# First expert's share added in mid-pass, decodes kept off one change of pass, one sum kept in PSUM, and an earlier load of the tail's tokens

## The chip, the cores and the metric

The kernel runs on one core of one Trainium2 chip. The metric is the device time of one execution in microseconds (us). The kernel before took 1981.72 us, the median of three runs (1981.59 to 1982.14).

## The reference

Three layers follow each other. Block-causal attention over 4 batches of 8 heads, 576 positions and width 64 gives 2304 tokens of width 512. A mixture of 8 experts follows: a gate matrix P comes from eight rounds of row and column normalising, and each expert adds its weighted output:

```python
for e in range(E):
    h = np.maximum(x @ w1[e], 0.0)
    ye = h @ w2[e]
    out += P[:, e:e + 1] * ye
```

A last layer computes `h = x @ w_in`, a softmax of h times h, a normalisation scaled by `g_ln`, and a product with `w_out`. The inputs `w_in`, `w_out` and `g_ln` belong to this last layer.

## The kernel before

All products are made from two parts of each number, a rounded high part and the rest, so that one product takes three matmuls. Expert 0 is computed beside the attention. Its result y, not yet weighted, is held in DRAM (`ydram`) for the last 1536 tokens.

Experts 1 to 7 are split in halves, the units u = 2 to 15, and the tokens are worked in three **passes** of 768 tokens, p = 0, 1 and 2. In every unit the first layer is a fast 2x2 product scheme: seven half-size products instead of eight, named "1" to "7" (`first_layer`, L712). Their sums are formed by VectorE in banks a, b and c of PSUM, for two column groups g. Here `plus` (L717) adds a PSUM bank and a saved tile, and writes to a new SBUF tile or to a given place. For product "5" it writes a tile `vu3` in SBUF, and `hidden` (L759, in pass 0 L748) reads that tile.

In passes 1 and 2 the second layer uses seven products as well. `weighted_hidden` (L755) multiplies by the gate weights `Pb`, forms seven operand tiles R with differences on GpSimd and VectorE (L773) and splits them in two parts (ScalarE L769, GpSimd L770). `second_products` (L804) then makes the seven products of the unit before, and VectorE adds each into a running sum, `summed(f)` (L816; the first unit copies on ScalarE, L814). All of these sums stay in SBUF for a whole pass. TensorE has six PSUM banks of the pool `l1p` for the banks a, b and c and for three of four second-layer outputs (`yps`), and two banks of `mm`.

At the end of a pass `finish_pass` (L827) combines the seven sums by seven adds (L831, four on VectorE and three on GpSimd). It then loads the four blocks of y from `ydram` (L846), weights them on GpSimd (L848), adds them on VectorE (L850) and stores the result to `rdram` (L851). It runs once pass 1 is complete, when unit 2 of pass 2 is already under way, and once at the end of pass 2. The new pass cannot overwrite a sum before that sum has been combined and stored.

The weights of the last layer arrive as 64-bit numbers and are **decoded** in 32 pieces (`decode`, L455): a load, seven or eight VectorE instructions (L465 to L485), a split by ScalarE and GpSimd (L445, L446) and a store to `wdram` (L488). `late_decode(n)` (L972) does one piece at each n from 8 to 39, where n counts units: n = 0 to 13 is pass 0, 14 to 27 pass 1, 28 to 41 pass 2. So 27 is unit 15 of pass 1, and 28 and 29 are units 2 and 3 of pass 2. At a change of pass `spread_x` (L590) also prepares the new tokens X.

The **tail** is the last layer over 18 tiles of 128 tokens. It loads decoded `w_in` (`wi`, L1025), the first tokens (`xin` with two buffers, L1028 and L1049, from `adram`), decoded `w_out` (`wo`, L1034), and from tile 6 on tokens from `rdram` (L1055). `early(t)` transposes and splits tile t, `front` multiplies by `w_in` into one of two PSUM tiles `big` and computes the softmax and the normalisation, `turn` transposes, `back` multiplies by `w_out`. The small tiles of `front` come from a pool `mp` whose memory is taken over from the pools of the passes, the sums "5", "6" and "7" among them.

All DMAs that matter here are issued by one queue, SP. The order of the instructions on every engine, SP's included, is fixed when the program is built: a scheduler takes the program's order as priority and its own model of when things are ready. On the chip each engine and SP work strictly in that order.

Of the kernel before, what the change touches and what calls it, by code (L numbers as in the profile page):

```python
# [24 lines left out]
def build(ctx, tc, qT, kT, v, w_gate, w1, w1s, w2, w_in, w_out, g_ln, out):  # L25
# [686 lines left out]
    def first_layer(W, X, hidden):  # L712

        bank = {}
        tmp = {}

        def plus(g, name, a, to=None):  # L717
            if to is None:
                to = tmp[g, name] = tmpp.tile([P, BLK], F32, tag=name, name=name)
            nc.vector.tensor_tensor(to, bank[g, a], tmp[g, "r1" if a == "b" else name[1:]], op=ALU.add)  # L720
            return to


        plan = (("1", "a"), ("6", "b"), ("2", "a"), ("7", "b"), ("5", "c"), ("4", "b"), ("3", "c"))
        for i, a in plan:
            start, stop = i in "165", i in "243"
            for g in range(2):
                if start:
                    bank[g, a] = l1p.tile([P, 512], F32, tag="l1", name=f"ps{a}")[:, 0:BLK]
                product(W[i], X[i], bank[g, a], g, start, stop)  # L730
                if i == "1":
                    t = tmp[g, "r1"] = tmpp.tile([P, BLK], F32, tag="r1", name="r1")
                    nc.scalar.copy(t, bank[g, "a"])
                elif i == "6":
                    plus(g, "u2", "b")
                elif i == "2":
                    hidden(g, 1, 1, bank[g, "a"])
                elif i == "7":
                    plus(g, "u3", "b")
                elif i == "5":  # L740
                    hidden(g, 2, 2, plus(g, "vu3", "c"))
                elif i == "4":
                    hidden(g, 2, 1, plus(g, "v", "b", bank[g, "b"]))
                else:
                    hidden(g, 1, 2, plus(g, "vu2", "c", bank[g, "c"]))
# [73 lines left out]
    def gate_weights(e, p):  # L819

        t = pbp.tile([P, 2 * BLK], F32, tag="pb", name="pb")
        nc.sync.dma_start(
            t.rearrange("p (t q) -> p t q", q=P), pdram[6 * p : 6 * p + 6, e, :].partition_broadcast(P)
        )
        return t

    def finish_pass(p):  # L827


        def add(eng, o, a):  # L830
            eng.tensor_tensor(summed(o), summed(o), summed(a), op=ALU.add)  # L831

        v, g = nc.vector, nc.gpsimd
        add(g, "2", "1")
        add(v, "6", "1")
        add(v, "7", "6")
        add(g, "6", "5")
        add(v, "4", "7")
        add(v, "7", "5")
        add(g, "3", "6")  # L840
        Pb = gate_weights(0, p)

        for f, i, j in (("4", 1, 1), ("7", 1, 0), ("2", 0, 1), ("3", 0, 0)):
            y = hb.tile([P, 2, BLK], F32, tag="hb", name="y0")
            n0 = (2 * (p - 1) + j) * BLK
            nc.sync.dma_start(y, ydram[:, 2 * i : 2 * i + 2, n0 : n0 + BLK])  # L846
            w = Pb[:, None, j * BLK : (j + 1) * BLK].to_broadcast([P, 2, BLK])
            g.tensor_tensor(y, y, w, op=ALU.mult)  # L848
            s = summed(f).rearrange("p (k n) -> p k n", k=2)
            v.tensor_tensor(s, s, y, op=ALU.add)  # L850
            nc.sync.dma_start(rdram[:, 2 * i : 2 * i + 2, n0 : n0 + BLK], s)  # L851

    def second_layer(u, p, ws, hs):
        e = u // 2
# [108 lines left out]
    for i in range(16):  # L963
        for half in range(2):

            if i < 8:
                a = i % 2 * 1024 + half * 512
                late.append((i, half, w_in[i // 2 * P : i // 2 * P + P, a : a + 512]))
            else:
                c = i - 8  # L970
                late.append((i, half, w_out[c * P : c * P + P, half * 512 : half * 512 + 512], gsc[:, c : c + 1]))
    def late_decode(n):  # L972
        if 8 <= n < 40:
            decode(*late[n - 8])


    ws = second_weights(2)
# [21 lines left out]
    for n, (p, u) in enumerate([*work, (3, 2)]):  # L999
        if n < len(work):  # L1000
            if u % 2 == 0:
                Pb = gate_weights(u // 2, p)
            R = {}
            hidden, steps = weighted_hidden(R, Pb)
            first_layer(W, X, hidden)
            late_decode(n + 14)

        if before:
            for _ in second_products(*before):
                next(steps, None)  # L1010
        run(steps)
        if n < len(work):
            if n + 1 < len(work):
                if work[n + 1][0] > p:
                    X = {}
                    run(spread_x(p + 1, X))
                W = load_factors(work[n + 1][1], 0)
            before = load_factors(u, 1), R, u == 2
        if u == 2 and p > 1:
            finish_pass(p - 1)  # L1020
    rctx.close()
    wip = ctx.enter_context(tc.tile_pool(name="wip", bufs=8, side="right"))
    xin = ctx.enter_context(tc.tile_pool(name="xin", bufs=2, side="right"))
    w2p = ctx.enter_context(tc.tile_pool(name="w2p", bufs=8, side="right"))
    wi = [[load_decoded(wip, 2 * dc + f) for f in range(2)] for dc in range(4)]  # L1025
    early0 = [xin.tile([P, DM], F32, tag="x", name="xin") for t in range(2)]
    for t in range(2):
        nc.sync.dma_start(early0[t], adram[:, t * DM : t * DM + DM])  # L1028
    ectx.close()
    lctx.close()  # L1030
    mm2 = ctx.enter_context(tc.tile_pool(name="mm2", bufs=2, space=PSUM, side="left"))
    big = ctx.enter_context(tc.tile_pool(name="big", bufs=2, space=PSUM, side="left"))
    wop = ctx.enter_context(tc.tile_pool(name="wop", bufs=8, side="left"))
    wo = [load_decoded(wop, 8 + c) for c in range(8)]  # L1034


    mp = ctx.enter_context(tc.tile_pool(name="mp", bufs=3, side="left"))
# [2 lines left out]

    def early(t):
        x2 = w2p.tile([P, 2, 4, P], F32R, tag="w", name="x2")
        if t < 2:
            x = early0[t]
        else:
            x = xin.tile([P, DM], F32, tag="x", name="xin")
        if t < 6:
            if t > 1:
                nc.sync.dma_start(x, adram[:, t * DM : t * DM + DM])  # L1049
            src = mm.tile([P, 4, P], F32, tag="mm", name="xtp")  # L1050
            for c in range(4):
                nc.tensor.transpose(src[:, c, :], x[:, c * P : c * P + P], ident)
        else:
            src = x.rearrange("p (c q) -> p c q", c=4)
            nc.sync.dma_start(src, rdram[:, :, (t - 6) * P : (t - 5) * P])  # L1055
        nc.scalar.copy(x2[:, 0], src)
        nc.vector.tensor_tensor(x2[:, 1], src, r32(x2[:, 0]), op=ALU.subtract)
        return x2
# [67 lines left out]
    xs = [early(t) for t in order[:2]]  # L1126
    lns, lts = [], []
    for i in range(NT + 4):
        if i + 2 < NT:
            xs.append(early(order[i + 2]))  # L1130
        if i < NT:
            lns.append(front(order[i], xs[i]))
        if 3 <= i < NT + 3:
            lts.append(turn(*lns[i - 3]))
        if i >= 4:
            back(order[i - 4], lts[i - 4])
# [45 lines left out]
```

## Time and profile before

| what | value |
|---|---|
| median of three runs | 1981.72 us |
| the profiled execution, its own time | 1983.74 us |
| its span in the trace | 1982.0 us |
| VectorE busy | 1454.0 us, 73% of the span |
| GpSimd busy | 1163.6 us, 59% |
| ScalarE busy | 743.3 us, 38% |
| mean granted TensorE clock | 0.985 |

The span is what the rows of the trace cover; the profiled execution's own time has 1.74 us around it. PE is TensorE's matmuls, PEld its weight loads, DVE is VectorE, ACT ScalarE, POOL GpSimd, SP the queue that issues DMAs. In a row of a timeline the first number is the start in us, the second the length. Square brackets hold the idle time of the engine just before, and what ended it.

### The profile page before, as it was taken

The page shows a single profiled execution, that of the slowest core. Times are in us where ns is not written, and L with a number is a line of the kernel's source. Part 1 is how long each engine was busy: PE and PEld are TensorE (multiplying, and loading weights), DVE is VectorE, ACT ScalarE, POOL GpSimd, SP SyncE. Part 2 cuts the span into 40 slices and gives each one's busy share as a digit, 9 for nine tenths or more (in the row PEclk, how much of TensorE's full clock was granted, in tenths as well). Part 3 has the DMA queues.
Part 4 walks back from the last instruction along what each step waited for, and adds up shares of the span by engine and source line. Part 5 has one row for each costly group of instructions (what it writes and reads, how often), then busy time and mean ns, then how long its engine had stood idle before and what let it go on. Part 6 is the DMA issues. An engine that isn't in the chain of part 4 may idle for free.

```text
span 1982.0 us, 31143 instructions
## 1 busy us (share of the span) xinstructions
PE 1898.4 (96%) x10487; PEld 1762.7 (89%) x10487; DVE 1454.0 (73%) x3104; ACT 743.3 (38%) x1555; POOL 1163.6 (59%) x920
## 2 busy tenths in 40 slices
PE   5899999889999999999999999998999999989999
PEld 4688998788998989889999999987999999978887
DVE  5868677666777769888867667797866766678774
ACT  5766657433434434343222222222222122224332
POOL 7775645455766667656666676668757557631000
PEclk8999999999999999999999999998999999989999
DMA  8765554337888888879787787876788787851100
GB/s 233 189 181 150 153 148 117 134 99 270 298 303 309 292 315 311 297 251 370 271 289 265 272 279 257 288 259 238 282 285 294 257 278 274 307 205 44 47 28 32
DMA packets 197758, 454.61 MB, mean 229 GB/s; under 512 B 20432, under 2 KB 78432, under 8 KB 197472
## 3 DMA queue, kind: packets, MB, share of 16 engines
q1 hardware_dynamic: 197600, 452.63, 67.3%
q8 instruction: 84, 1.38, 0.3%
q14 instruction: 74, 0.61, 0.1%
HBM read 295.72 MB, written 128.52 MB: 214 GB/s over the span
## 4 chain that ended last, share of the span: by engine, by line
PE 77%; DVE 9%; DMA 4%; POOL 4%; issue 3%; ACT 1%; SPq 1%; DVEq 0%; POOLq 0%; ACTq 0%
PE yps L708 5%; PE yps L710 5%; PE yps L709 5%; PE psb L709 4%; PE psb L708 4%; PE psb L710 4%; PE yps L862 3%; PE yps L864 3%; PE yps L863 3%; PE psc L710 2%; PE psc L708 2%; PE psc L709 2%; PE psa L708 2%; PE psa L710 2%; PE psa L709 2%
## 5 line engine op out<-in xcount | busy, mean ns | idle before, releaser
L770 POOL TENSOR_TENSOR hf<-hb,hf 128x768 fp32r<-128x768 f32 x196 | 368.4, 1895 | 94.9 <-ACT hf L769 94.9
L769 ACT CAST hf<-hb 128x768 fp32r<-128x768 f32 x196 | 160.5, 836 | 490.4 <-POOL hb L773 158.5
L708 PE MATMUL yps<-hf,W 128*128 128x384 f32 x784 | 268.1, 342 | 10.5 <-DVE hb L762 8.2
L709 PE MATMUL yps<-hf,W 128*128 128x384 f32 x784 | 267.1, 341 | 0.0
L710 PE MATMUL yps<-hf,W 128*128 128x384 f32 x784 | 263.8, 341 | 0.0
L773 POOL TENSOR_TENSOR hb<-hb 128x768 f32<-128x768 f32 x84 | 158.8, 1891 | 161.6 <-DVE hb L762 160.1
L816 DVE TENSOR_TENSOR acc<-yps,acc 128x384 f32<-128x384 f32 x364 | 192.6, 549 | 67.6 <-PE yps L710 66.9
L446 POOL TENSOR_TENSOR w<-raw,w 128x512 fp32r<-128x512 f32 x96 | 125.8, 1323 | 109.3 <-ACT w L445 104.6
L708 PE MATMUL psb<-X,W 128*128 128x384 f32 x504 | 169.7, 337 | 1.4 <-ACT acc L814 1.4
L709 PE MATMUL psb<-X,W 128*128 128x384 f32 x504 | 169.3, 336 | 0.0
L710 PE MATMUL psb<-X,W 128*128 128x384 f32 x504 | 167.7, 335 | 0.0
L708 PEld LDWEIGHTS yps<-hf,W 128*128 128x128 f32 x784 | 149.0, 190 | 13.1 <-DVE hb L762 9.8
L709 PEld LDWEIGHTS yps<-hf,W 128*128 128x128 f32 x784 | 149.1, 190 | 0.0
L720 DVE TENSOR_TENSOR u<-psb,r 128x384 f32<-128x384 f32 x168 | 91.1, 550 | 79.1 <-PE psb L710 71.4
L710 PEld LDWEIGHTS yps<-hf,W 128*128 128x128 f32 x784 | 148.7, 190 | 0.0
L862 PE MATMUL yps<-w,h 128*128 128x512 f32 x336 | 133.3, 397 | 5.5 <-DVE acc L868 2.7
L233 POOL TENSOR_SCALAR e<-e,sv 128x128 f32<-128x128 f32 (+2 forms) x144 | 81.1, 567 | 95.6 <-DVE sv L229 31.4
L446 POOL TENSOR_TENSOR W<-raw,W 128x512 fp32r<-128x512 f32 x84 | 117.7, 1416 | 29.7 <-ACT W L445 29.7
L864 PE MATMUL yps<-w,h 128*128 128x512 f32 x336 | 132.6, 395 | 0.0
L863 PE MATMUL yps<-w,h 128*128 128x512 f32 x336 | 132.5, 394 | 0.0
L1102 POOL TENSOR_SCALAR lh<-ln 128x1024 f16<-128x1024 f32 x18 | 19.1, 1059 | 187.4 <-DVE ln L1099 65.2
L708 PE MATMUL psa<-X,W 128*128 128x384 f32 x336 | 113.5, 338 | 2.9 <-ACT W L445 1.5
(233 smaller groups left out, 5330.5 us busy)
## 6 DMA issues: line engine op xcount, KB each, us to landing
W<-fd SPq DMA_DIRECT2D x392, 512.0 KB, 5.6
fd<-W SPq DMA_DIRECT2D x154, 512.0 KB, 5.2
fd<-w SPq DMA_DIRECT2D x84, 256.0 KB, 4.7
raw<-in_w1s SPq DMA_DIRECT2D x56, 256.0 KB, 5.5
raw<-in_w SPq DMA_DIRECT2D x14, 1024.0 KB, 6.9
raw<-in_w SPq DMA_DIRECT2D x40, 256.0 KB, 3.4
kh<-khigh SPq DMA_DIRECT2D x64, 144.0 KB, 2.9
kl<-kraw SPq DMA_DIRECT2D x64, 144.0 KB, 2.7
```

Of the source, the lines that this page charges most:

```text
L446: nc.gpsimd.tensor_tensor(t[:, 1, :], raw, r32(t[:, 0, :]), op=ALU.subtract)
L708: nc.tensor.matmul(ps, wh, xl, start=start and kc == 0, stop=False, skip_group_check=True)
L709: nc.tensor.matmul(ps, wh, xh, start=False, stop=False, skip_group_check=True)
L710: nc.tensor.matmul(ps, wl, xh, start=False, stop=stop and kc == 1, skip_group_check=True)
L720: nc.vector.tensor_tensor(to, bank[g, a], tmp[g, "r1" if a == "b" else name[1:]], op=ALU.add)
L769: nc.scalar.copy(hi, a)
L770: nc.gpsimd.tensor_tensor(lo, a, r32(hi), op=ALU.subtract)
L773: eng.tensor_tensor(o, a, b, op=ALU.subtract)
L816: nc.vector.tensor_tensor(a, ps, a, op=ALU.add)
L862: nc.tensor.matmul(ps, hl, ws[c][:, 0, :], start=c == 0, stop=False)
L863: nc.tensor.matmul(ps, hh, ws[c][:, 1, :], start=False, stop=False)
L864: nc.tensor.matmul(ps, hh, ws[c][:, 0, :], start=False, stop=c == 3)
```

## The change

The added y moves out of `finish_pass` into a new generator `first_expert_sums`, which adds y, weighted on GpSimd, to the running sums while units 4 to 7 of the pass are worked, one block to a unit, all on GpSimd. One block goes into two sums, because the later combination would otherwise count it twice. The decode leaves out n = 27, 28 and 29; it begins at 7 and ends at 41. The sum after product "5" is written back into bank a of PSUM. The tail loads tokens of six tiles from `adram` ahead of `wi`, with six buffers, and `wo` stands later in the program, in the second round of the tail's loop.

```diff
-                    hidden(g, 2, 2, plus(g, "vu3", "c"))
+                    hidden(g, 2, 2, plus(g, "vu3", "c", bank[g, "a"]))
...
         add(g, "3", "6")
+        for f, i, j in (("4", 1, 1), ("7", 1, 0), ("2", 0, 1), ("3", 0, 0)):
+            n0 = (2 * (p - 1) + j) * BLK
+            nc.sync.dma_start(
+                rdram[:, 2 * i : 2 * i + 2, n0 : n0 + BLK], summed(f).rearrange("p (k n) -> p k n", k=2)
+            )
+
+    def first_expert_sums(p):
+
         Pb = gate_weights(0, p)
-        for f, i, j in (("4", 1, 1), ("7", 1, 0), ("2", 0, 1), ("3", 0, 0)):
+        for i, j, to in ((0, 1, (("2", ALU.add),)), (1, 1, (("4", ALU.add),)),
+                         (0, 0, (("3", ALU.add),)), (1, 0, (("5", ALU.add), ("3", ALU.subtract)))):
             y = hb.tile([P, 2, BLK], F32, tag="hb", name="y0")
...
-            g.tensor_tensor(y, y, w, op=ALU.mult)
-            s = summed(f).rearrange("p (k n) -> p k n", k=2)
-            v.tensor_tensor(s, s, y, op=ALU.add)
-            nc.sync.dma_start(rdram[:, 2 * i : 2 * i + 2, n0 : n0 + BLK], s)
+            nc.gpsimd.tensor_tensor(y, y, w, op=ALU.mult)
+            for f, op in to:
+                s = summed(f).rearrange("p (k n) -> p k n", k=2)
+                nc.gpsimd.tensor_tensor(s, s, y, op=op)
+            yield
...
+    when = [n for n in range(7, 42) if n not in (27, 28, 29)][:32]
+
     def late_decode(n):
-        if 8 <= n < 40:
-            decode(*late[n - 8])
+        if n in when:
+            decode(*late[when.index(n)])
...
         run(steps)
+        if u == 4 and p < 3:
+            adding = first_expert_sums(p)
+        if n < len(work) and 4 <= u < 8:
+            next(adding)
...
-    xin = ctx.enter_context(tc.tile_pool(name="xin", bufs=2, side="right"))
+    xin = ctx.enter_context(tc.tile_pool(name="xin", bufs=6, side="right"))
     w2p = ctx.enter_context(tc.tile_pool(name="w2p", bufs=8, side="right"))
+    xa = []
+    for t in range(6):
+        xa.append(xin.tile([P, DM], F32, tag="x", name="xin"))
+        nc.sync.dma_start(xa[t], adram[:, t * DM : t * DM + DM])
     wi = [[load_decoded(wip, 2 * dc + f) for f in range(2)] for dc in range(4)]
-    early0 = [xin.tile([P, DM], F32, tag="x", name="xin") for t in range(2)]
-    for t in range(2):
-        nc.sync.dma_start(early0[t], adram[:, t * DM : t * DM + DM])
...
-    wo = [load_decoded(wop, 8 + c) for c in range(8)]
...
     for i in range(NT + 4):
+        if i == 1:
+            wo = [load_decoded(wop, 8 + c) for c in range(8)]
         if i + 2 < NT:
             xs.append(early(order[i + 2]))
```

## Rows read from the trace of the kernel before

**Rows 1.** The page, busy time of the engines over the whole span.

```profile
PE 1898.4 (96%) x10487; PEld 1762.7 (89%) x10487; DVE 1454.0 (73%) x3104; ACT 743.3 (38%) x1555; POOL 1163.6 (59%) x920
```

**Rows 2.** Windows: length, busy time (instructions) by engine, granted clock, DMA share.

```profile
1100.00:1129.20 29.20, 29.20 (x169) 29.20 (x168) 20.30 (x40) 7.13 (x10) 19.00 (x12) 1.00 0.69 238
1276.00:1310.00 34.00, 30.18 (x157) 28.47 (x157) 33.93 (x52) 11.66 (x21) 26.04 (x17) 0.95 0.75 246
1340.00:1376.00 36.00, 26.91 (x126) 25.22 (x125) 32.40 (x32) 7.46 (x14) 32.65 (x18) 0.86 0.59 215
1700.00:1745.00 45.00, 45.00 (x260) 44.97 (x259) 28.18 (x51) 8.65 (x12) 31.86 (x18) 1.00 0.82 296
1745.00:1775.00 30.00, 21.60 (x96) 16.88 (x95) 22.35 (x43) 8.19 (x14) 8.06 (x4) 0.83 0.68 245
```

**Rows 3.** Waits between 1330 and 1380 us: total, times, longest.

```profile
PE yps L708 <- DVE hb L762: 8.0, 3, 4.3
```

**Rows 4.** Groups on VectorE, 1340 to 1376 us: busy, mean ns.

```profile
L850 DVE TENSOR_TENSOR acc<-acc,y 128x768 f32<-128x768 f32 x4 | 7.8, 1941 | 0.0
L762 DVE SCALAR_TENSOR_TENSOR hb<-vu,pb 128x384 f32<-128x384 f32 x2 | 4.4, 2188 | 1.4 <-POOL hf L770 1.4
...
L471 DVE SCALAR_TENSOR_TENSOR a<-w,a 128x256 uint32<-128x256 uint32 x1 | 2.0, 2019 | 0.0
...
L485 DVE TENSOR_SCALAR f<-f,gsc 128x256 f32<-128x256 f32 x1 | 0.3, 346 | 0.0
```

**Rows 5.** Groups on GpSimd in the same stretch, 1340 to 1376 us.

```profile
L848 POOL TENSOR_TENSOR y<-y,pb 128x768 f32<-128x768 f32 x4 | 8.0, 2012 | 0.0
```

**Rows 6.** Groups on VectorE, 1276 to 1310 us, different shapes apart.

```profile
L477 DVE CUSTOM_DVE_ANT_0 a<-a,b 128x512 uint16<-128x512 uint16 x1 | 2.0, 2024 | 0.0
...
L465 DVE TENSOR_SCALAR a<-w 128x256 uint32<-128x256 uint32 x1 | 0.3, 280 | 0.0
```

**Rows 7.** VectorE between 1757 and 1771 us, in order of time.

```profile
1756.16 1.81 DVE L850 TENSOR_TENSOR acc<-acc,y 128x768 f32<-128x768 f32 x2
...
1766.32 0.06 DVE L1039 MEMSET magic<- 128x1 uint32 x1 [0.96 <-DMA rd<-acc]
1766.33 2.36 DVE L1069 TENSOR_REDUCE nm<-h 128x1 f32<-128x1024 f32 x2
```

**Rows 8.** TensorE between 1760.5 and 1775 us, in order of time.

```profile
1760.68 0.39 PE L1067 MATMUL h<-w,x 128*128 128x512 f32 x1
1762.75 1.27 PE L1052 MATMUL xtp<-ident,xin 128*128 128x128 f32 x8 [1.67 <-DMA xin<-ad]
1767.98 1.09 PE L1052 MATMUL xtp<-ident,xin 128*128 128x128 f32 x4 [3.96 <-DMA xin<-ad]
1770.78 0.77 PE L1065 MATMUL h<-w,x 128*128 128x512 f32 x1 [1.71 <-DVE sm L1074]
```

**Rows 9.** SP between 1745 and 1770 us: DMA issues in order.

```profile
1747.65 3.96 SPq L492 DMA_DIRECT2D w<-wd  x8
...
1754.80 4.53 SPq L851 DMA_DIRECT2D rd<-acc  x4
```

**Rows 10.** Issue to landing of the decoded weights' 16 loads (L492).

```profile
DMA to landing us min/median/max: 3.5/9.5/10.9
```

**Rows 11.** Issue to landing of the eight stores of finished sums (L851).

```profile
DMA to landing us min/median/max: 2.4/8.4/10.6
```

**Rows 12.** Groups on VectorE, 1050 to 1250 us, in mid-pass.

```profile
L762 DVE SCALAR_TENSOR_TENSOR hb<-vu,pb 128x384 f32<-128x384 f32 x13 | 14.0, 1077 | 0.4
...
L762 DVE SCALAR_TENSOR_TENSOR hb<-psa,pb 128x384 f32<-128x384 f32 x14 | 7.8, 556 | 5.3 <-PE psa L710 5.2
```

**Rows 13.** Groups on VectorE, 500 to 800 us, in pass 0.

```profile
L751 DVE SCALAR_TENSOR_TENSOR h<-vu,h 128x384 fp32r<-128x384 f32 x18 | 26.6, 1496 | 0.2
```

**Rows 14.** Groups on GpSimd, 1050 to 1250 us, in mid-pass.

```profile
L773 POOL TENSOR_TENSOR hb<-hb 128x768 f32<-128x768 f32 x21 | 39.0, 1857 | 55.8 <-DVE hb L762 55.8
```

**Rows 15.** VectorE between 1128 and 1137 us, one first layer in mid-pass.

```profile
1129.78 0.56 DVE L762 SCALAR_TENSOR_TENSOR hb<-psa,pb 128x384 f32<-128x384 f32 x1 [0.48 <-PE psa L710]
...
1134.75 0.56 DVE L762 SCALAR_TENSOR_TENSOR hb<-vu,pb 128x384 f32<-128x384 f32 x1
```

**Rows 16.** TensorE in the same first layer.

```profile
1132.87 0.34 PE L708 MATMUL yps<-hf,W 128*128 128x384 f32 x1
```

More of the change, by code (lines that the diff above doesn't have):

```diff
@@ L1042, in early @@
         x2 = w2p.tile([P, 2, 4, P], F32R, tag="w", name="x2")
[L1043 to L1046, printed above, removed]
         if t < 6:
-            if t > 1:
-                nc.sync.dma_start(x, adram[:, t * DM : t * DM + DM])
+            x = xa[t]
             src = mm.tile([P, 4, P], F32, tag="mm", name="xtp")
@@ L1053, in early @@
         else:
-            src = x.rearrange("p (c q) -> p c q", c=4)
+            src = xin.tile([P, DM], F32, tag="x", name="xin").rearrange("p (c q) -> p c q", c=4)
             nc.sync.dma_start(src, rdram[:, :, (t - 6) * P : (t - 5) * P])
```

## The prediction, made before the changed kernel was built or run

> **What bounds the kernel now.** I read the page first: TensorE is busy 96% of the span [rows 1], so a gain can only come from stretches where it is not, or where its clock is down. The windows show where these are [rows 2]. In mid-pass 169 matmuls take 29.20 us, 0.173 us each, with VectorE busy 20.30 and GpSimd 19.00 of it; the last 45 us of pass 2 run at the same 0.173. VectorE there has about 9 us of slack in each unit, so work that is added or removed in mid-pass should cost or give nothing by itself. Three stretches fall short:
>
> - 1276 to 1310 us (unit 15 of pass 1 with the spreading of X): 157 matmuls, worth 157 x 0.173 = 27.1 us, in 34. So 6.9 us are lost, and VectorE is busy 33.93 of the 34 [rows 2].
> - 1340 to 1376 us (the change from pass 1 to 2): 126 matmuls, worth 21.8 us, in 36. So 14.2 us are lost. VectorE is busy 32.40, GpSimd 32.65, and the granted clock is 0.86 [rows 2]. The waits say who ended TensorE's pauses: VectorE's L762, which frees PSUM banks, 8.0 us in three waits up to 4.3 [rows 3]. The clock falls to its lower level after such pauses, which the 14.2 us include.
> - The opening of the tail, 1745 to 1775, at a mean granted clock of 0.83 [rows 2]. From the last matmul of the second tile (1760.68) to the first of the third (1770.78) there are 10.1 us, with only twelve transposes between [rows 8].
>
> Together some 30 us, or 1.5% of the time. This measurement can tell about 0.2% (4 us) from no change.
>
> **The change, part by part.** The sum is made against the profiled execution, 1983.74 us, which lies 2.02 us above the median of the runs; I take the same gain off the median.
>
> *A, no decode in unit 15 of pass 1 (n = 27).* Eight VectorE instructions, from 2.0 down to 0.3 us, 8.0 us in all, leave a stretch in which VectorE has no idle time [rows 2, 6]. At most the whole 6.9 us come back. The rest of the stretch, the fourteen splits of X, remains uneven, so I take 5, with bounds 3 and 6.9. The decode's ScalarE, GpSimd and store steps go with it; those engines have idle time there.
>
> *B, the change of pass.* Three things leave VectorE between 1340 and 1376: four adds of y, 7.8 us; eight decode instructions of n = 29 between 2.0 and 0.3 us, 11.2 us; and the excess of the two reads of `vu`, 2.188 us against 0.556 for the same instruction on a PSUM bank, 3.3 us [rows 4, 12]. That is 22.3 of 32.4 busy us. GpSimd loses four multiplications, 8.0 of 32.65 us [rows 5]. SP loses four loads of y and their wait, and the stores of the sums come sooner, so ScalarE's copies into these sums are released sooner. What is late next: the seven adds that combine the sums stay, and the first copies of the new pass wait for them and their stores. I take 12 of 14.2, with bounds 8 (the adds still end too late for half of it) and 14.2.
>
> First the row: an L850 add took 1.94 us on average beside a busy GpSimd, and a `vu` read 2.19 [rows 4]. The Trainium skill ("SBUF — State Buffer", Who interferes with whom) says that a VectorE instruction with two SBUF inputs and a GpSimd instruction that reads SBUF exclude each other for a whole instruction. By that, emptying GpSimd would also shorten the adds that stay, and B would be 14 rather than 12; the rows agree in kind. The same sentence speaks against the mid-pass work, which is among the rivals.
>
> *C, the tail.* The third tile's matmuls wait for a `big` buffer, which the first tile's reduction (L1069) begins to free. It starts at 1766.33, right after a memset that ended a wait for the stores to `rd`, and TensorE restarts 4.45 us later [rows 7, 8]. Those stores are issued from 1754.80 on, after the y adds (the last ended at 1757.97), and behind eight `wo` loads issued from 1747.65 on [rows 7, 9]. The loads landed up to 10.9 us after issue, so by about 1762; a store takes 2.4 us on an emptier queue and up to 10.6 on a full one [rows 10, 11]. With the y adds gone, stores can be issued some 4 us sooner. If they still stand behind the eight loads, they land soon after 1762 and the gain is about 3. If they stand ahead, the reduction can start before the second tile ends, and all but the transposes of the 10.1 us comes back, about 9. I take 4, near the first: `wo` is later in the program, but its memory is free at the same moment, and SP's order goes by when a load is ready. Bounds 1 and 9. The early tokens (six loads of 256 KB, four of them new at that place, ahead of `wi`) end TensorE's two waits for them, 1.67 and 3.96 us [rows 8], but these lie inside the same pause and are not counted twice. `wi` comes later by these 1 MB, against which the 1.6 MB of y no longer stand there.
>
> *D, the y work in mid-pass.* Per pass nine GpSimd instructions of the size of L773, 1.86 us each, 16.7 us, spread over four units: 3.7 or 5.6 us in each [rows 14], plus four loads and one load of gate weights on SP. GpSimd's 19.00 of 29.20 us become at most 24.6 [rows 2]. Cost 0, hidden by TensorE's own work; if that cover were gone, up to 33 us for both passes.
>
> *E, `vu` in PSUM and the moved decodes.* A `vu` read falls from 1.08 to 0.56 us in passes 1 and 2, and from 1.50 in pass 0 [rows 12, 13], 28 times in each pass. TensorE is the bound there, so I count 0, with bounds -1 and +2 us. The three decodes move to unit 9 of pass 0 and to the last two units of pass 2, where VectorE is busy 28.18 of 45 us [rows 2]: 0.
>
> Sum: 5 + 12 + 4 = 21, with bounds 12 and 30. So 1962.7 us for a profiled execution and **1960.7 us** for the median.
>
> **The rivals.**
>
> 1. *The change of pass keeps half of its pause.* The seven adds, their stores and the copies that wait for them stay in a row, and GpSimd still holds some 24 us of work in 36 [rows 2, 5]. Then B gives 4, and A and C 2 each: 8, or 1973.7 us. For it: seven adds and the split of R still meet there. Against it: 22.3 us of VectorE's work is gone. Chance 0.15.
> 2. *Slower by PSUM.* Bank a is now held from the read after product "2" (1129.78) until the read after "5" (1134.75), 5 us longer [rows 15]. In this time TensorE starts second-layer products of another PSUM bank at 1132.87 [rows 16]. If no bank of the six is left, it stands still until the read ends. At one product of six matmuls, 1.04 us, in each of the 28 units of passes 1 and 2, that is 29 us, and 21 less 29 gives 8 us slower, 1990 us. It decides from 0.75 us in each unit on. Against it: TensorE's order is made for the new holds, other products of the first layer can take the place, and the read itself is shorter. Chance 0.08.
> 3. *Slower by GpSimd in mid-pass.* Its 18 new instructions delay VectorE's or the operands R. In full, 33 us less the 21, 1994 us; it decides if more than 21 of the 33 reach TensorE. Against it: 24.6 of 29.2 us at most. Here the Trainium skill's rule (same section) would let each GpSimd instruction hold up one of VectorE's; no row in mid-pass shows TensorE waiting for that. Chance 0.03.
> 4. *It does nothing measurable*: the scheduler puts other late work in the freed places, and the pauses stay. 1981 us. Chance 0.04.
>
> **How the numbers follow.** The forecast has 0.70, with a range of its own from 1952 to 1969. The range given reaches from the full sum of the three losses (30, 1951) to just above the first rival, 1976; it leaves out rivals 2 to 4, 0.15, and a little at the ends. Faster is the forecast and rival 1, 0.85; same is rival 4, 0.04; slower is rivals 2 and 3, 0.11.
>
> **What would show it right or wrong.** Windows of the same two units at the change of pass should hold 0.173 to 0.18 us per matmul with the clock near 1.00 and VectorE well below full (A, B). The groups L848 and L850 should be gone from there, and GpSimd's new groups in units 4 to 7 should stand beside a full TensorE (D). L762 on bank a should read 0.55 us (E). The first L1069 should start about 3 us earlier after the last second-layer product than now (C). The prediction is wrong if mid-pass takes more than 29.3 us per unit (rivals 2 and 3), or if TensorE still waits over 5 us for L762 or the sums at the change of pass (rival 1). A first L1069 that starts before the second tile's matmuls end would put the time near 1955.

## The result, and the profile after

The changed kernel took 1995.66 us (median of six runs, 1990.12 to 2001.80) against 1981.93 for the kernel before (six runs, 1981.18 to 1984.52): a ratio of 1.0068, interval 1.0048 to 1.0089. It is **slower by 14 us**; the forecast was 21 faster. The profiled execution has a span of 1996.6 us. The page's first part, against [rows 1]:

```profile
PE 1901.9 (95%) x10487; PEld 1764.5 (88%) x10487; DVE 1392.9 (70%) x3096; ACT 741.4 (37%) x1555; POOL 1164.3 (58%) x930
```

VectorE has lost 61 us of work and TensorE has as many instructions as before, so the time did not come from more work. To see where it came from, cut both spans at the same points of the work: the starts of ScalarE's first copy (L733) of units n = 0, 13, 16, 27, 31 and 41. Windows between these points, of the kernel before and of the changed one (length, busy time and instructions by engine, granted clock, DMA share, GB/s):

```profile
851.30:948.90 97.60, 93.23 (x479) 86.46 (x480) 81.92 (x121) 34.15 (x68) 61.58 (x42) 0.98 0.86 315
948.90:1271.20 322.30, 321.79 (x1839) 320.83 (x1838) 231.72 (x443) 79.00 (x114) 208.56 (x121) 1.00 0.79 273
1271.20:1411.90 140.70, 127.31 (x680) 123.12 (x679) 121.13 (x172) 38.66 (x70) 103.12 (x58) 0.95 0.74 260
1411.90:1704.20 292.30, 292.13 (x1672) 291.74 (x1671) 203.70 (x403) 69.16 (x101) 193.30 (x112) 1.00 0.79 278
```

```profile
858.00:956.40 98.40, 89.08 (x451) 82.41 (x450) 74.16 (x116) 33.89 (x68) 62.99 (x43) 0.97 0.84 307
956.40:1289.30 332.90, 326.52 (x1848) 323.68 (x1847) 224.49 (x444) 77.79 (x113) 226.89 (x131) 0.99 0.78 272
1289.30:1415.00 125.70, 120.71 (x678) 119.50 (x677) 87.30 (x144) 38.71 (x66) 91.62 (x52) 0.99 0.78 274
1415.00:1721.40 306.40, 298.14 (x1673) 294.13 (x1673) 209.16 (x410) 69.22 (x101) 206.64 (x120) 0.99 0.76 266
```

The third line of each is the change from pass 1 to 2: 140.7 us became 125.7, with 678 matmuls where 680 stood. That gain came. But the middles of passes 1 and 2 (second and fourth lines), which were full before, take 10.6 and 14.1 us more, and pass 0, which lies before these windows, 8.7 more. In the two middles TensorE's pauses make up 6.4 and 8.3 us, where they were 0.5 and 0.2, and its own busy time has grown by 4.7 and 6.0 us at nearly the same number of matmuls. A unit of the middles now takes 30.3 and 30.6 us, over the 29.3 that the prediction had set as the sign that it is wrong.

These stages, in us, for the kernels of this study (one profiled execution each; the stretch ahead of pass 0, which no edit touches but the copy in pb_rows' edit, takes 448.8 to 455.8 us, so differences of 2 or 3 us in one stage mean little). `pb3` has no row, and its slow profiled execution (2337.74 us at a mean granted clock of 0.75) is left out of its time below, while the profiled executions of `pb_rows` and `from8` took 8 and 5 us more than these kernels' medians.

| kernel | pass 0 | 0 to 1 | middle 1 | 1 to 2 | middle 2 | tail |
|---|---|---|---|---|---|---|
| before | 400.5 | 97.6 | 322.3 | 140.7 | 292.3 | 277.8 |
| after | 409.2 | 98.4 | 332.9 | 125.7 | 306.4 | 275.2 |
| y_alone | 399.3 | 95.9 | 328.3 | 134.0 | 298.9 | 276.2 |
| d_alone | 400.8 | 96.8 | 320.9 | 128.7 | 293.8 | 280.7 |
| p_alone | 401.6 | 97.5 | 322.2 | 140.8 | 296.2 | 279.6 |
| t_alone | 398.8 | 95.9 | 322.6 | 140.3 | 292.8 | 279.8 |
| no_p | 401.8 | 99.4 | 325.3 | 125.1 | 299.9 | 275.7 |
| no_y | 406.4 | 96.0 | 323.9 | 130.6 | 299.2 | 279.7 |
| no_d | 401.6 | 97.1 | 331.1 | 135.5 | 300.0 | 275.9 |
| pb_rows | 411.0 | 94.9 | 324.2 | 119.8 | 296.6 | 274.6 |
| mm_first | 411.0 | 98.4 | 328.1 | 118.7 | 299.6 | 275.6 |
| from8 | 402.0 | 97.7 | 330.8 | 131.1 | 301.9 | 275.6 |
| p_first | 401.6 | 100.6 | 323.8 | 134.1 | 293.6 | 277.8 |
| pbrows_before | 399.5 | 95.9 | 321.6 | 139.2 | 291.9 | 279.4 |
| pbrows_no_p | 401.2 | 96.6 | 323.2 | 119.1 | 293.9 | 276.1 |
| cured | 401.8 | 93.0 | 324.6 | 121.1 | 295.5 | 277.7 |

The waits name what is new. TensorE's waits over the whole span of the changed kernel (engine, tile and line, what was waited for: total, times, longest):

```profile
...
PE yps L708 <- DMA W<-fd: 14.8, 5, 5.1
...
PE yps L872 <- DVE acc L878: 6.3, 3, 3.1
PE psb L708 <- DVE u L720: 5.6, 4, 2.3
PE h L1077 <- DVE e L1089: 4.6, 1, 4.6
```

At the change of pass the wait of [rows 3] is gone. In its place TensorE waits for **second-layer weights W** that have not landed, for 10.2 of these 14.8 us in the two middles. The longest such wait, around 1087 us, in windows:

```profile
1077.00:1084.00 7.00, 7.00 (x41) 6.82 (x41) 3.19 (x7) 1.74 (x3) 7.00 (x5) 1.00 0.86 301
1084.00:1090.00 6.00, 0.93 (x6) 0.63 (x5) 2.83 (x6) 1.56 (x2) 4.07 (x3) 0.71 0.96 357
1090.00:1097.00 7.00, 7.00 (x32) 7.00 (x33) 3.56 (x9) 0.00 (x0) 1.28 (x1) 0.76 0.41 151
1097.00:1104.00 7.00, 7.00 (x42) 7.00 (x41) 7.00 (x12) 1.68 (x2) 5.80 (x4) 1.00 0.87 276
```

TensorE stands for 5.1 us, and then works 7 us at a granted clock of 0.76, in which it does 32 matmuls instead of 41: another 9 x 0.171 = 1.5 us. SP in the same stretch, in order of time (start, length, line, load, count):

```profile
1068.06 0.37 SPq L822 DMA_DIRECT2D pb<-pd  x1
1068.52 0.49 SPq L634 DMA_DIRECT2D W<-fd  x1
...
1070.16 4.15 SPq L634 DMA_DIRECT2D W<-fd  x3
1074.40 0.66 SPq L822 DMA_DIRECT2D pb<-pd  x1
1079.54 5.03 SPq L634 DMA_DIRECT2D W<-fd  x5
```

Two loads of gate weights (`pb`, L822) stand 6.3 us apart. There are 16 over the whole kernel in both versions; but the two for the added y stood in `finish_pass` and now stand here. Issue to landing, of the four weight loads between 1066 and 1076 us, and of all `pb` loads of this kernel:

```profile
DMA to landing us min/median/max: 8.9/9.7/10.6
...
DMA to landing us min/median/max: 7.3/8.4/12.7
```

All weights of mid-pass 1 land in 5.2 us by the median, and in the kernel before in 5.3. But there, too, the weights right behind a gate-weight load land late: those issued within 6 us after one in 9.1 us by the median, here in 9.7. So the slow landing is not new. New are two such stretches next to each other, and a weight that is wanted sooner. With each load matched to its first matmul, the weight that ends the 5.1 us wait was issued at 1080.0, landed at 1089.7 and was used at 1089.8; in pass 2 two landed at 1517.3 and 1520.5 and were used at 1517.5 and 1520.7. In the two middles (950 to 1280 and 1420 to 1740 us) of the kernel before no second-layer weight is used less than 3 us after it landed, and in the changed kernel 12 and 10 are, nearly all of them the 2nd or the 4th of their unit. This count, **late weights**, is given with the runs below.

### The profile page after: what moved, and what is told of

Read it like the earlier page. It is cut to its first block, busy times and chain, and to the rows that moved or that the text cites. A ratio compares the mean times of both kernels' runs of the same rounds, so it can differ in the third digit from the quotient of the medians.

```text
span 1996.6 us, 31135 instructions
## 1 busy us (share of the span) xinstructions
PE 1901.9 (95%) x10487; PEld 1764.5 (88%) x10487; DVE 1392.9 (70%) x3096; ACT 741.4 (37%) x1555; POOL 1164.3 (58%) x930
## 4 chain that ended last, share of the span: by engine, by line
PE 76%; DMA 8%; DVE 7%; POOL 4%; issue 3%; ACT 1%; SPq 1%; POOLq 0%; ACTq 0%; DVEq 0%
PE yps L708 6%; PE yps L709 6%; PE yps L710 6%; PE psb L708 3%; PE psb L709 3%; PE psb L710 3%; PE yps L872 3%; PE yps L873 3%; PE yps L874 3%; PE psa L708 2%; PE psa L710 2%; PE psa L709 2%; PE psc L708 2%; PE psc L709 2%; PE psc L710 2%
## 5 line engine op out<-in xcount | busy, mean ns | idle before, releaser
L770 POOL TENSOR_TENSOR hf<-hb,hf 128x768 fp32r<-128x768 f32 x196 | 365.1, 1879 | 74.7 <-ACT hf L769 73.7
L708 PE MATMUL yps<-hf,W 128*128 128x384 f32 x784 | 267.3, 343 | 18.9 <-DMA W<-fd 14.8
L446 POOL TENSOR_TENSOR w<-raw,w 128x512 fp32r<-128x512 f32 x96 | 125.7, 1323 | 121.8 <-ACT w L445 108.5
L446 POOL TENSOR_TENSOR W<-raw,W 128x512 fp32r<-128x512 f32 x84 | 113.7, 1369 | 24.8 <-ACT W L445 24.8
```

What stands on the lines that cost most here:

```text
L446: nc.gpsimd.tensor_tensor(t[:, 1, :], raw, r32(t[:, 0, :]), op=ALU.subtract)
L708: nc.tensor.matmul(ps, wh, xl, start=start and kc == 0, stop=False, skip_group_check=True)
L770: nc.gpsimd.tensor_tensor(lo, a, r32(hi), op=ALU.subtract)
```

## The experiments

**Each part alone.** `y_alone`: the added y in mid-pass and nothing else.

```diff
-        for f, i, j in (("4", 1, 1), ("7", 1, 0), ("2", 0, 1), ("3", 0, 0)):
-            y = hb.tile([P, 2, BLK], F32, tag="hb", name="y0")
...
+        if u == 4 and p < 3:
+            adding = first_expert_sums(p)
+        if n < len(work) and 4 <= u < 8:
+            next(adding)
```

> Only the mid-pass adding of y, all else as before. Theory DMA (the extra gate-weight load makes two broadcast loads fall within some 6 us, weights W land late): mid-pass stalls on W as in the changed kernel, about +20 us over passes 1 and 2, less some 5 us at the change of pass and 2 in the tail: 1990 to 2000 us. Rival PSUM (the lost time comes from the sum kept in bank a): no mid-pass stall here, 1970 to 1978 us.

Measured: 1987.91 us, ratio 1.0025 (1.0015 to 1.0034). The change of pass gives back 6.7 us, and the middles lose 6.0 and 6.6, though late weights are only 1 and 3. Here another load is late. VectorE stands for the raw data of a decode, whose load was issued behind two gate-weight loads and their weights, and the instruction that TensorE's operands come from (L762, then the split by ScalarE and GpSimd) stands behind that decode. In pass 2, VectorE and then TensorE:

```profile
1513.56 0.29 DVE L465 TENSOR_SCALAR a<-w 128x256 uint32<-128x256 uint32 x1 [6.12 <-DMA w<-in_w_out]
...
1513.97 0.55 DVE L762 SCALAR_TENSOR_TENSOR hb<-vu,pb 128x384 f32<-128x384 f32 x1
...
1516.23 0.66 PE L708 MATMUL yps<-hf,W 128*128 128x384 f32 x1 [4.18 <-issue]
```

The longest such wait of VectorE in the middles is 3.2 us in the kernel before and 6.1 here. Once in pass 1 TensorE also waits 2.2 us for GpSimd's split (L770).

`d_alone`: the decodes alone.

```diff
+    when = [n for n in range(7, 42) if n not in (27, 28, 29)][:32]
-        if 8 <= n < 40:
-            decode(*late[n - 8])
+        if n in when:
+            decode(*late[when.index(n)])
```

> Only the decodes moved (first at n = 7, none at 27 to 29, last at 41). Theory DMA: passes 1 and 2 gain 8 to 12 us at the change of pass, pass 0 loses 2 to 5 for a seventh decode: 1972 to 1978 us. Rival PSUM: the same here, but without the loss in pass 0: 1970 to 1973 us. Rival order (any change reshuffles the order on all engines and costs by itself): 1985 us or more.

Measured: 1978.23 us, 0.9972 (0.9963 to 0.9981). The change of pass is 12.0 us shorter and the tail 2.9 longer.

`p_alone`: the sum in PSUM alone.

```diff
-                    hidden(g, 2, 2, plus(g, "vu3", "c"))
+                    hidden(g, 2, 2, plus(g, "vu3", "c", bank[g, "a"]))
```

> Only the sum after product 5 written to PSUM bank a. Theory DMA: nothing in passes 1 and 2, 0 to 3 us gained in pass 0: 1979 to 1983 us. Rival PSUM: TensorE lacks a bank for about 0.5 us in each of 28 units, and pass 0 loses too: 1992 to 2000 us, with waits on L720 or L762 in every unit.

Measured: 1993.41 us, 1.0056 (1.0041 to 1.0071). **The smallest edit costs the most**, 10 us, with 11 and 9 late weights. Its profile puts 3.9 us of it in the middle of pass 2; the rest lies in pieces of under 2.5 us. The change of pass is as long as before, but not by the same waits. Those for L762 fell from the 8.0 us of [rows 3], and weights that have not landed took their place:

```profile
PE yps L708 <- DMA W<-fd: 4.4, 2, 4.0
...
PE yps L708 <- DVE hb L762: 1.9, 3, 1.0
```

`t_alone`: the tail's loads alone.

```diff
-    xin = ctx.enter_context(tc.tile_pool(name="xin", bufs=2, side="right"))
+    xin = ctx.enter_context(tc.tile_pool(name="xin", bufs=6, side="right"))
...
-    wo = [load_decoded(wop, 8 + c) for c in range(8)]
...
+        if i == 1:
+            wo = [load_decoded(wop, 8 + c) for c in range(8)]
```

> Only the tail's loads moved. Both theories: the stores of the sums still wait for the y adds, and the reduction of the first tile starts as late as before less a little: 1979 to 1982 us.

Measured: 1982.92 us, 0.9999 (0.9988 to 1.0009). In its tail the waits for tokens [rows 8] are gone, and one wait of the same stretch has become longer:

```profile
PE h L1060 <- DVE sm L1069: 9.4, 1, 9.4
```

Alone it gives nothing: TensorE still waits for the reduction, behind the y adds.

**All but one part.** `no_p`: the changed kernel without the sum in PSUM.

```diff
-                    hidden(g, 2, 2, plus(g, "vu3", "c", bank[g, "a"]))
+                    hidden(g, 2, 2, plus(g, "vu3", "c"))
```

> The changed kernel with the sum of product 5 in SBUF again. Theory PSUM (the alone run of that edit cost 10 us, so it costs here as well): 1984 to 1988 us, and pass 0 back at some 400 us. Theory DMA (late W loads in mid-pass carry the loss): the mid-pass stalls stay, 1992 to 1998 us.

Measured: 1978.84 us, 0.9973 (0.9963 to 0.9982), 17 us less than the changed kernel. Late weights 2 and 1, and VectorE's longest wait for a decode's raw data is still 5.9 us. Pass 0, middle 1 and middle 2 come back by 7.4, 7.6 and 6.5 us.

`no_y`: the changed kernel without the added y in mid-pass; it stands in `finish_pass` again.

```diff
-        if u == 4 and p < 3:
-            adding = first_expert_sums(p)
-        if n < len(work) and 4 <= u < 8:
-            next(adding)
```

> The changed kernel with y added at the end of the passes again, so that no y load and no extra gate-weight load stands in mid-pass. Theory DMA: passes 1 and 2 come back by some 17 us in mid-pass and lose some 6 at the change of pass: 1982 to 1987 us. Theory PSUM: little changes, 1994 to 2000 us.

Measured: 1990.85 us, 1.004 (1.0024 to 1.0057). Late weights 12 and 11, as in the changed kernel, yet the middles lose only 1.6 and 6.9 us. Late weights come with the held bank; the added y turns them into longer waits.

**The gate-weight load.** `pb_rows`: the changed kernel with the gate weights stored by expert, so that each partition's 768 values are one row of 3 KB in DRAM and not six of 512 bytes. The copy that brings P into this order stands once, before pass 1.

```diff
-    pdram = dram.tile([NT, E, P], F32, name="pd")
+    pdram = dram.tile([E, NT, P], F32, name="pd")
...
+        nc.vector.tensor_copy(pc, prT)
...
-            t.rearrange("p (t q) -> p t q", q=P), pdram[6 * p : 6 * p + 6, e, :].partition_broadcast(P)
+            t, pdram[e, 6 * p : 6 * p + 6, :].rearrange("t q -> (t q)").partition_broadcast(P)
```

> The changed kernel, with the gate weights laid out in DRAM so that each partition reads one row of 3 KB instead of six of 512 bytes (the same bytes, one sixth of the packets). Theory DMA: a gate-weight load lands in 3 to 5 us instead of 8 to 12, W loads behind it no longer come late, and 10 to 17 us come back: 1979 to 1986 us. Theory PSUM: within 3 us of the changed kernel, 1992 to 1999 us.

Measured: 1970.77 us, 0.9941 (0.9921 to 0.9962), **25 us less than the changed kernel** and 12 less than the one before. Late weights 2 and 2, no wait for a weight over 1 us; only pass 0 remains long (411.0).

`pb3`: the changed kernel with a third buffer for gate weights.

```diff
-    pbp = ectx.enter_context(tc.tile_pool(name="pbp", bufs=2, side="left"))
+    pbp = ectx.enter_context(tc.tile_pool(name="pbp", bufs=3, side="left"))
```

> The changed kernel with three buffers for gate weights instead of two, so that the extra load does not push the next two together. Theory DMA, if the bunching is what counts: 1985 to 1990 us. If the extra load's own time counts, or the PSUM bank: 1993 to 1999 us.

Measured: 1996.28 us, 1.0068 (1.0046 to 1.0089): nothing gained. But the edit did not do what it was made for: in its trace the two gate-weight loads still stand 7.7 us apart in pass 1 and 5.9 in pass 2, where the changed kernel has 6.3 and 4.9. So this run does not tell what their nearness costs.

**Which weights TensorE takes.** The order of its instructions shows why the bank matters. With bank a held longer, no bank of `l1p` is free for second-layer products in the middle of a first layer: a, b and c for two groups are all six. The scheduler fills in those products whose output lies in the `mm` banks, and by `n % 4 == 3` these are the sums 3, 7 and 11: the 2nd, 4th and 6th weight of a unit. They are taken some 10 us ahead of their place. `mm_first` gives the `mm` banks to the sums 0 and 1, which use the first weight of a unit, and to the sum 8, which uses the fifth:

```diff
-                pool, tag = (mm, "mm") if n % 4 == 3 else (l1p, "l1")
+                pool, tag = (mm, "mm") if n in (0, 1, 8) else (l1p, "l1")
```

> The changed kernel, with one thing else: of the 14 second-layer sums of a unit the three that go to the mm banks are the sums 0, 1 and 8 (before: 3, 7 and 11), so the weights that can fill TensorE while bank a is held are the first second-layer weight of the unit, which land first, not the second, fourth and sixth. Theory DMA (the held bank only changes which weights TensorE takes first, and those have not landed): the weights are used in order again, hardly any is used less than 3 us after it landed, the middle stretches of passes 1 and 2 come back by 8 us each of the 10.6 and 14.1 that they lost, 1980 us (1976 to 1986). Rival PSUM (what costs is that a bank is held at all): nothing comes back, 1994 to 1998 us.

Measured: 1984.21 us, 1.0 (0.9986 to 1.0014), 11 us less than the changed kernel, with the bank kept by the same instructions. Late weights 0 and 0. The middles come back by 4.8 and 6.8 us, less than the 8 expected, and the change of pass, where a weight had been late by 4.6 us, by 7.0. Of what the middles still lose, part is the other load, as in y_alone: VectorE stands, before a decode, for its raw data, and L762, which frees a bank, stands behind it (start, length, then in brackets the idle time before it and its cause):

```profile
1098.31 0.30 DVE L465 TENSOR_SCALAR a<-w 128x256 uint32<-128x256 uint32 x1 [6.34 <-DMA w<-in_w_in]
...
1098.72 0.55 DVE L762 SCALAR_TENSOR_TENSOR hb<-psa,pb 128x384 f32<-128x384 f32 x1
```

`p_first` is p_alone with the same edit.

> The kernel before with the sum kept in PSUM, and the sums 0, 1 and 8 in the mm banks; nothing else of the change. Theory DMA (alone, the held bank costs only by the order of the weights): no weight is used less than 3 us after it landed in the middle of passes 1 and 2, 1983 us (1980 to 1986), 10 us less than the sum in PSUM alone. Rival PSUM (part of the 10 us is the held bank itself): 1988 us or more.

Measured: 1986.16 us, 1.0024 (1.0011 to 1.0036), late weights 0 and 0. About 7 of p_alone's 10 us are gone with the late weights, and 2 to 3 us remain open. That the order of the weights was most of the price is likely, not shown: 6.7 us of the difference between the two profiles lie in the change of pass, which p_alone had not made longer than before, and the banks' edit was not run on the kernel before, where it might gain by itself.

**Pass 0.** `no_d`: the changed kernel with the decodes where they were.

```diff
-        if n in when:
-            decode(*late[when.index(n)])
+        if 8 <= n < 40:
+            decode(*late[n - 8])
```

> The changed kernel without its moved decodes (the decode of unit n stands at n from 8 to 39 again); the added y, the sum in PSUM and the tail's loads stay. Theory (pass 0 loses its 8 us only where the held bank and the moved decodes meet: neither alone lengthens it): pass 0 is back at 401 us (399 to 403), the change from pass 1 to 2 is about 5 to 8 us longer than in the changed kernel, the middles stay long: 1993 us (1989 to 1997). Rival (pass 0 loses it to something else of the change, the added y's instructions or the buffers' places): pass 0 stays at 407 to 411 us, 2000 us or more.

Measured: 1994.77 us, 1.0055 (1.004 to 1.007). Pass 0 is back at 401.6. TensorE's waits in pass 0, in no_d and in the changed kernel:

```profile
PE psa L708 <- ACT W L445: 1.4, 1, 1.4
PE yps L872 <- DVE acc L878: 1.1, 2, 0.6
PE psa L708 <- ACT r L733: 1.1, 1, 1.1
```

```profile
PE yps L872 <- DVE acc L878: 3.2, 2, 1.9
PE yps L872 <- DVE h L751: 3.1, 2, 3.0
...
```

These waits are 5.0 of the 7.6 us between the two. One of them on VectorE and then on TensorE, in the changed kernel in order of time:

```profile
813.59 1.03 DVE L465 TENSOR_SCALAR a<-w 128x256 uint32<-128x256 uint32 x1
814.54 1.39 DVE L474 TENSOR_SCALAR b<-w 128x256 uint32<-128x256 uint32 x1
815.85 1.50 DVE L468 SCALAR_TENSOR_TENSOR a<-w,a 128x256 uint32<-128x256 uint32 x1
817.28 0.55 DVE L720 TENSOR_TENSOR psc<-psc,u 128x384 f32<-128x384 f32 x1
817.75 1.02 DVE L471 SCALAR_TENSOR_TENSOR a<-w,a 128x256 uint32<-128x256 uint32 x1
...
820.10 0.54 DVE L751 SCALAR_TENSOR_TENSOR h<-psb,h 128x384 fp32r<-128x384 f32 x1
...
820.70 0.80 PE L872 MATMUL yps<-w,h 128*128 128x512 f32 x1 [2.98 <-DVE h L751]
```

Some 6 us of decode stand ahead of the h that TensorE waits for. `from8` asks whether it is the decode that begins one unit early:

```diff
-    when = [n for n in range(7, 42) if n not in (27, 28, 29)][:32]
+    when = [n for n in range(8, 42) if n not in (27, 28)]
```

> The changed kernel, its decodes at n = 8 to 41 but for 27 and 28 (changed kernel: 7 to 41 but for 27, 28 and 29), so that pass 0 has its decodes where the kernel before has them and the last unit of pass 1 still has none. Theory (the decode that begins one unit early puts VectorE's long operations ahead of the h that the second layer of pass 0 waits for, once the bank is held): pass 0 is back at 401 us (399 to 403), the change from pass 1 to 2 keeps 9 us or more of its 15, the middles stay long: 1988 us (1984 to 1992). Rival (pass 0 loses it to where the later decodes stand or to the added y): pass 0 stays at 407 us or more, 1995 to 2000 us.

Measured: 1990.05 us, 1.0042 (1.0023 to 1.006). Pass 0 is at 402.0 with the last unit of pass 1 and the first of pass 2 still free of decodes: it was the early start, which adds a decode at n = 7 and shifts every piece of pass 0 by one unit, and only where the bank is held too (p_alone 401.6, d_alone 400.8, both 406 to 411). Why the shift costs this much beyond waits like the one above is not shown.

**The cures together.** `pbrows_before`: the kernel before with pb_rows' edit alone.

> The kernel before, with the gate weights stored as one row of 3 KB per partition and nothing else. Theory DMA: in the kernel before a second-layer weight is used 8 us or more after it landed, so a faster gate-weight load frees nothing: 1982 us (1979 to 1984). Rival (the gate-weight load itself delays the kernel before, as its change from pass to pass waits for one): the change of pass is shorter by 5 us or more and pass 0 to 1 by 2, 1975 us (1972 to 1978).

Measured: 1980.44 us, 0.9982 (0.9971 to 0.9993). The faster load by itself is worth 3 us. The 8 us of the expectation is too high, though: some second-layer weights of the kernel before are used about 5 us after landing, the median being 11.

`pbrows_no_p`: the added y, the decodes and the tail's loads, with pb_rows' edit and without the sum in PSUM.

> The changed kernel without the sum kept in PSUM and with the gate weights stored so that a partition's 768 are one row of 3 KB in DRAM (one piece per partition where six of 512 bytes stood). Theory DMA: both of the things that make a weight late are gone, the middle of passes 1 and 2 stands as in the kernel before (within 3 us each), the change of pass keeps its 14 us, and pass 0 is back at 401 us: 1964 us (1960 to 1970). Rival order (the additions on GpSimd and VectorE cost the middle of a pass, whatever the loads do): the middle of pass 2 keeps 5 us of the 7.6 that it still loses without the sum in PSUM, 1974 us (1971 to 1978).

Measured: **1961.61 us, 0.9888 (0.9873 to 0.9902)**, 22 us less than the kernel before and the best version of this study. No wait of VectorE for a decode's raw data in its middles is over 1.9 us. Its windows of the middle of pass 1, the change to pass 2 and the middle of pass 2:

```profile
948.00:1271.20 323.20, 321.61 (x1839) 320.78 (x1838) 238.30 (x444) 78.09 (x113) 228.78 (x132) 1.00 0.81 278
1271.20:1390.30 119.10, 118.91 (x678) 118.12 (x677) 92.88 (x144) 38.88 (x65) 91.48 (x51) 1.00 0.83 284
1390.30:1684.20 293.90, 293.22 (x1678) 292.67 (x1677) 210.69 (x410) 69.08 (x102) 206.43 (x120) 1.00 0.80 279
```

TensorE is full in all three, the change of pass included. Issue to landing of its `pb` loads (L824 here):

```profile
DMA to landing us min/median/max: 4.2/5.6/7.0
```

`cured`: all four parts, with the edits of pb_rows, mm_first and from8.

> All four parts of the change, with the gate weights as rows of 3 KB, the sums 0, 1 and 8 in the mm banks, and the decodes at n = 8 to 41 but for 27 and 28. Theory (late weights and the early decode of pass 0 are all that the change loses): pass 0 at 401 us, the middles within 3 us of before, the change from pass 1 to 2 at 119 to 125 us, 1961 us (1956 to 1966), as the version without the sum in PSUM. Rival (the held bank has a price of its own): 1969 us or more.

Measured: 1965.44 us, 0.9919 (0.9897 to 0.9941). All four parts together are 18 us faster than the kernel before once these three causes are gone, and 3 of the 18 are what the faster load gives by itself. The sum in PSUM is not needed for it: the version without is at least as fast.

## Why the prediction was wrong

**A and B held.** 5 + 12 us were expected; the change of pass became 15.0 us shorter, with one late weight still in it (4.6 us). In pbrows_no_p it is 21.6 us shorter, above the bounds' sum of 21.1; 1.5 of this comes with the gate load alone. TensorE's waits in this stage, in the kernel before (1271 to 1412 us) and in the changed one (1289 to 1415):

```profile
PE yps L708 <- DVE hb L762: 8.0, 3, 4.3
PE yps L708 <- DVE acc L816: 2.3, 1, 2.3
...
```

```profile
PE yps L708 <- DMA W<-fd: 4.6, 1, 4.6
...
```

Rival 1, half of the pause kept, did not happen. Whether the rule of the Trainium skill ("SBUF — State Buffer", Who interferes with whom), by which B would be 14 and not 12, has a share in the 21.6 was not tried apart.

**C was 4 and is about 3.** The first reduction stood 62.1 us after the start of the last unit [rows 7: 1766.33 less 1704.2], and stands 58.1 after it now; TensorE's third tile begins 3.0 us earlier by the same measure (66.6 and 63.6). The tail is 2.6 us shorter, which alone would be within what a stage varies. VectorE and TensorE there:

```profile
1779.49 0.06 DVE L1056 MEMSET magic<- 128x1 uint32 x1 [3.67 <-DMA rd<-acc]
1779.50 2.35 DVE L1081 TENSOR_REDUCE nm<-h 128x1 f32<-128x1024 f32 x2
...
1784.98 0.77 PE L1077 MATMUL h<-w,x 128*128 128x512 f32 x1 [4.60 <-DVE e L1089]
```

As expected, the stores still end the wait: the reduction stands behind them.

**D is the step that failed first: "four loads and one load of gate weights on SP. ... Cost 0, hidden by TensorE's own work".** The GpSimd work was hidden but for little. It is there as counted, in groups between 1020 and 1140 us,

```profile
L860 POOL TENSOR_TENSOR acc<-acc,y 128x768 f32<-128x768 f32 x3 | 5.5, 1865 | 0.0
L857 POOL TENSOR_TENSOR y<-y,pb 128x768 f32<-128x768 f32 x2 | 3.7, 1864 | 0.0
```

and with the gate load changed to rows and the bank free the middles cost 0.9 and 1.6 us (pbrows_no_p), so rival 3 is worth at most 2.5 us here. The loads were not hidden: I had looked at whether TensorE, VectorE and GpSimd had room, and not at how long after its landing each thing behind the added load is used, the second-layer weights and the raw data of the decodes. VectorE's 9 us of slack in a unit do not help an instruction that stands behind one whose data is missing. The added y alone cost 12.6 us in the middles, the same work without the sum in PSUM (no_p) 10.6, and beside the faster load 2.5. The four loads of y are in all of these versions; what they cost apart from the added gate-weight load was not tried.

**E is the step that failed most: "TensorE is the bound there, so I count 0, with bounds -1 and +2 us".** The read did become 0.55 us, as expected (0.554, 28 of them between 1050 and 1250 us), and it bought nothing. The longer hold of bank a cost 10 us alone and 17 beside the other parts. Rival 2 had the right place, and its time, 1990 us, is near by luck, for its mechanism is not what happened: of TensorE's 14.6 us of pauses in the two middles 10.6 are waits for weights and 3.2 for a bank. As I wrote against that rival, other products took the place; they were second-layer products in the `mm` banks, out of order, and their weights had not landed. mm_first keeps the bank in the same way and has no late weight.

"The three decodes move to unit 9 of pass 0 and to the last two units of pass 2 ...: 0" failed too: every decode of pass 0 moved, not one, and with the bank held this cost 7 to 10 us there.

So 17.6 us of the forecast 21 were gained (15.0 and 2.6), and 33.4 lost (8.7 + 10.6 + 14.1) in places that I had put at 0. The losses do not add up part by part: the order of the weights and the slow gate load each leave slack that the other uses up. Of the 24.7 us of the middles the faster load brings back 18.5, and the other order of the weights 11.6.

**What stays open.** The 2 to 3 us that p_first keeps, and what the banks' edit would do to the kernel before; where the rest of p_alone's 10 us lies beside the 3.9 in the middle of pass 2, as no other stage of its profile is over 2.5 us longer; and the price of the added gate-weight load apart from that of the y loads.

## What to carry to other kernels

Before an added load is called hidden, list the loads behind it on its queue with the time between landing and first use, and ask whether another part of the change shortens that time. A longer hold of a PSUM bank cost little at the bank here: look at which work the scheduler then takes instead, and whether its operands are there. When a change is slower, undo its parts one by one: here one line held a gain of 17 us, and the layout of the gate weights one of 25.

## What was not expected of the hardware

A `pb` load of 384 KB landed after 8.4 us by the median (7.3 to 12.7) as six pieces of 512 bytes per partition, and after 5.6 (4.2 to 7.0) as one row of 3 KB. The weights behind it gained as well: those issued within 6 us after one landed in 6.3 us by the median and not in 9.7. The pages count the packets, of the changed kernel and of pbrows_no_p:

```profile
DMA packets 197757, 454.60 MB, mean 228 GB/s; under 512 B 20432, under 2 KB 78432, under 8 KB 197472
```

```profile
DMA packets 187517, 454.60 MB, mean 232 GB/s; under 512 B 20432, under 2 KB 66144, under 8 KB 187232
```

The bytes are equal, and 16 x 768 = 12288 packets of under 2 KB are gone. The Trainium skill ("DMA: Bandwidth & Descriptors", Why small descriptors are slow) gives a packet a fixed 3 cycles or so beside one for each 32 bytes, as the first of two mechanisms. By that one, an estimate from its figures, six packets of 512 bytes take 6 x (16 + 3) = 114 cycles and one of 3 KB 99, or 15% more. The trace has 50% more from issue to landing, so the measurement decides; the landing also holds the wait behind other loads, which this rule leaves out.

Two pauses of TensorE cost more than their length: after the 5.1 us at 1087 the granted clock was 0.76 for 7 us, and after the 2.98 us at 820 it was 0.50, the lower of its two levels, for 2.7 us:

```profile
820.70:823.40 2.70, 2.70 (x6) 2.15 (x7) 2.70 (x6) 1.00 (x2) 1.28 (x1) 0.50 1.03 419
```
